# First tokens loaded in three contiguous pieces, one set of column means for two units, norm factors by a power on GpSimd, and a new order of the loads and of the opening's steps

## The chip, the cores and the metric

The kernel runs on one core of one Trainium2 chip. The time is the device time of one execution in microseconds (us); each kernel is run several times and medians are compared. The profile is one profiled execution. Engines are named as the profile names them: PE (matrix products) and PEld (its weight loads), DVE (vector), ACT (scalar and activation), POOL (GpSimd), SP (the queue that issues most transfers).

## The reference

For an input x of 2048 tokens and 448 channels the output is g·a + (1 − g)·b, with g a sigmoid of a weighted sum of each token's channels. Branch a is a state-space convolution along the tokens plus a skip term. Branch b is a mixer; its beginning is what this change touches:

```python
h = _gelu(_layernorm(x, axis=-1) @ w1)          # 448 x 448
c = D // 4
# the four quarters of h are shifted along the tokens by +1, -1, +2, -2
hs = jnp.concatenate([g0, g1, g2, g3], axis=-1) @ w2
x1 = x + hs
h2 = _gelu(_layernorm(x1, axis=-1) @ w3) @ w4   # 448 x 1792, 1792 x 448
return x1 + h2
```

`_layernorm` takes a token's mean and divides by sqrt(variance + 1e-5). Everything is float32.

## The kernel before

The 2048 tokens are worked on in four blocks of 512 (`TB`). Every float32 operand is split into a high part (the value rounded for PE's fast float32 form) and a low part (the rest), and a product is made of three products of parts: high·high, high·low and low·high.

A block's mixer has "units". The four units of the first layer (n = 0, 1, 2, 3 of block 0 are the quarters g = 0, 2, 1, 3 of `w1`'s columns) each multiply 448 channels, in four slices k of 128 rows (the last holds 64), into a PSUM tile; `first` at L478 issues these products. The norm is not applied to the tokens. Instead each column of `w1` has its mean over the channels taken out of it (`center`, L937), which removes the tokens' means, and the result is multiplied by the tokens' factors 1/sqrt(variance + eps) afterwards. The factors (`r1`) are one column of 128 tokens per tile; PE turns them into rows (`rows_of`, L363). Then come the gelu on ACT and the second layer (`second`, L603) into four accumulators `acc`. After that the 14 units of the 1792-wide layers follow for each block in the same two functions.

The opening is block 0's first layer. Here nothing has been loaded or split yet, so its steps are cut small and written out by hand in one table, `ORDER`; `begin` walks it and issues each step in turn, and every engine works through its own instructions in exactly that order. Words of the table that matter here:

- `m2`, `m0`, `m1`, `m3`: the column means of a quarter, as plain float32 matmuls of a constant 1/448 with the raw weights `w1r`, result in `pm`. `wt` and `ws` are sums on DVE (L922, L924, L910) of slices of quarters 2 and 0, made so that those means take two and three matmuls in place of four.
- `c2`: take the means out (DVE); `h2`: the high part (ACT, L940); `l2`: the low part (DVE, L943); the same for 0, 1, 3. Quarter 2 has only 64 columns, and its high and low parts lie side by side in `w1d`.
- `xha`, `xla`, `xhb`, `xlb`: high (ACT, L956) and low part (DVE, L961 and L963) of the tokens, left half (a) and right half (b) of the block.
- `p1:x0a`: a product of unit 1, low tokens (x), slice 0, left half; `h` stands for high by high, `l` for high tokens by low weights. Whole words such as `s0:10` are second-layer products.
- `w`: a warm-up product of constants (`pw`, L903).
- `sa0` to `sa6`, `sb2` to `sb9`: mean and variance of a token tile on ACT (two passes, L981 and L983) or on DVE (L974, L976). `ra0`, `ra1`: the factors of tiles 0 to 4 and 5 to 8; `ra`, `rm`, `rn`: their transposes on PE.
- `xz`, `pe`, `sk`: two edge tokens; `ld`: issue the later loads; `wh`, `wl`: the parts of `w2`.

The first loads are issued by `first_loads` on two queues, SP's and ACT's. The first tokens, transposed and with their margins, come from the array `x0`, whose 128 rows hold the left half and then the right half of all four slices; the kernel takes from it the left half's slices 0 and 1, its slices 2 and 3, and the right half. The parts of `w1` are called u0a and u0b (two halves of quarter 0), u2, u1 and u3 below.

The factors are computed by nine small DVE steps, a first guess by an integer trick and two refinements (`rstd_ops`, L317 to L333), for the tiles of the opening. For most later sets `rstd` makes two of the steps on DVE and ten on POOL (L344 to L353).

Of the kernel before, what the change touches and what calls it, by code (L numbers as in the profile page):

```python
# [179 lines left out]
def mixer_and_small_steps(ctx, tc, xs, gg, okm, x, xT, xb, x0, w1, w2, w3, w4, gate, par, logdt, dskip, ident, out):  # L180
# [25 lines left out]
    one = big.tile([128, 1], F32, name="one")  # L206
    carry = big.tile([128, 4, 5], F32, name="carry")
# [47 lines left out]
    def first_loads():  # L255

        r = raw[0] = room([128, 4 * XW], "raw")
        parts0.append(r[:, :4 * HW].rearrange("p (k t) -> p k t", k=4))
        parts0.append(r[:, 4 * HW:].rearrange("p (k t) -> p k t", k=4))
        act, sp = nc.scalar.dma_start, nc.sync.dma_start  # L260

        def load_w1(queue, g):
            t = slice(W1O[g], W1O[g] + 4 * (GD if g == 2 else 128))
            queue(w1r[:, t], w1[:, t])

        load_w1(act, 2)
        sp(r[:, :2 * HW], x0[:, :2 * HW])
        act(w1r[:, :256], w1[:, :256])  # L268
        sp(w1r[:, 256:512], w1[:, 256:512])
        act(xs[:, 0, :], x[0:128])  # L270
        sp(r[:, 2 * HW:4 * HW], x0[:, 2 * HW:4 * HW])
        load_w1(sp, 1)
        load_x(1, 2)
        load_x(2, 3)
        load_w1(sp, 3)
        load_x(3, 5)
        sp(r[:, 4 * HW:], x0[:, 4 * HW:])
        sp(idt, ident)
        sp(w2r[:, 0], w2[:, 0])  # L279
        load_xt(1)  # L280
        sp(w2r[:, 1:4], w2[:, 1:4])
        load_x(NT + 1, 2 * NT + 1)

    def constants():
# [3 lines left out]
        nc.gpsimd.memset(one, 1.0)  # L288
        nc.gpsimd.memset(nu, 0.0)
# [22 lines left out]
    def rstd_ops(r, j0, j1):  # L312

        v, t = (wk.tile([128, NT + 1], F32, name=n)[:, :j1 - j0] for n in "vt")
        y = r[:, j0:j1]
        stt = nc.vector.scalar_tensor_tensor
        nc.vector.tensor_scalar(v, st[:, j0:j1, 1], EPS, None, op0=OP.add)  # L317
        yield
        nc.vector.tensor_scalar(y.bitcast(I32), v.bitcast(I32), -0.5, float(0x5f3759df), op0=OP.mult, op1=OP.add)
        yield  # L320
        nc.vector.tensor_mul(t, y, y)
        yield
        stt(t, t, -0.5 * 0.375, v, op0=OP.mult, op1=OP.mult)
        yield
        stt(y, t, 1.5 * 0.375, y, op0=OP.add, op1=OP.mult)
        yield
        nc.vector.tensor_mul(t, y, y)
        yield
        stt(t, t, 1.0 / 0.140625, v, op0=OP.mult, op1=OP.mult)
        yield  # L330
        stt(t, t, -10.0 / 3.0, t, op0=OP.add, op1=OP.mult)
        yield
        stt(y, t, 5.0, y, op0=OP.add, op1=OP.mult)  # L333
        yield

    def rstd(r, j0, j1, eng=nc.vector):
        if eng is nc.vector:
            drain(rstd_ops(r, j0, j1))
            return
        v, t = (wk.tile([128, NT + 1], F32, name=n)[:, :j1 - j0] for n in "vt")  # L340
        y = r[:, j0:j1]
        nc.vector.tensor_scalar(v, st[:, j0:j1, 1], EPS, None, op0=OP.add)
        nc.vector.tensor_scalar(y.bitcast(I32), v.bitcast(I32), -0.5, float(0x5f3759df), op0=OP.mult, op1=OP.add)  # L343
        eng.tensor_mul(t, y, y)  # L344
        eng.tensor_mul(t, t, v)
        eng.tensor_scalar(t, t, -0.5 * 0.375, 1.5 * 0.375, op0=OP.mult, op1=OP.add)
        eng.tensor_mul(y, y, t)
        eng.tensor_mul(t, y, y)
        eng.tensor_mul(t, t, v)
        eng.tensor_scalar(t, t, 1.0 / 0.140625, -5.0 / 3.0, op0=OP.mult, op1=OP.add)  # L350
        eng.tensor_mul(t, t, t)
        eng.tensor_scalar(t, t, 20.0 / 9.0, None, op0=OP.add)
        eng.tensor_mul(y, y, t)  # L353

    def rstd2(j0, j1):
        rstd(r2, j0, j1, nc.gpsimd if j0 < 3 * NT else nc.vector)
# [475 lines left out]
    def mean_bank(g):  # L832
        pm[g] = ps.tile([128, GD if g == 2 else 128], F32, name="pm", tag=("misc", "acc2", "acc1", "acc3")[g], bufs=1)
        return pm[g]
# [28 lines left out]
    def col_means(g):  # L863
        p = mean_bank(g)
        for k in range(4):
            c = int(k == 3)
            nc.tensor.matmul(p, cm[:, c:c + 1].to_broadcast([128, 128]), W1R[g][:, k, :], start=k == 0, stop=k == 3)
# [36 lines left out]

    WS = {}

    def presum():

        WS[1] = big.tile([128, 128], F32, name="ws", tag="lt")
        nc.vector.tensor_add(WS[1], W1R[0][:, 0, :], W1R[0][:, 1, :])  # L910

    def presum_mean():
        a, p = W1R[0], mean_bank(0)
        for q, (c, r) in enumerate(((1, a[:, 3, :]), (0, a[:, 2, :]), (0, WS[1]))):
            nc.tensor.matmul(p, cm[:, c:c + 1].to_broadcast([128, 128]), r, start=q == 0, stop=q == 2)

    def presum_unit2():

        a = W1R[2]
        v = big.tile([128, GD], F32, name="ws", tag="yt")  # L920
        WS[0] = v
        nc.vector.tensor_add(v, a[:, 0, :], a[:, 1, :])  # L922
        yield
        nc.vector.tensor_add(v, v, a[:, 2, :])  # L924
        yield

    def unit2_mean():

        p = mean_bank(2)
        for q, c in enumerate((1, 0)):  # L930
# [371 lines left out]
```

## Time and profile before

| | us |
|---|---|
| median of 3 runs (lowest, highest) | 371.17 (371.15, 371.31) |
| span of the profiled execution | 368.9 |
| PE busy in that span | 363.4 |
| DVE, ACT, POOL busy | 308.1, 215.9, 63.3 |

The profile gives the span from the first to the last instruction of one execution and no device time of its own for that execution; the span stands 2.27 us below the median of the timed runs. A row of the timeline gives the start in us from the span's beginning, the duration, the engine, the kernel's line, the operation, what is written and read, and in brackets how long the engine was idle before and what released it. Matmuls are pipelined: their durations overlap, so the distance from one start to the next is what one costs.

### The profile page before, as it was taken

How to read it: one execution, taken by the hardware profiler on the slowest of the kernel's cores; microseconds unless marked ns; L12 is line 12 of the kernel's file. 1: busy time of each engine (PE TensorE's matmuls, PEld its weight loads, DVE VectorE, ACT ScalarE, POOL GpSimd, SP SyncE). 2: the span in 40 equal slices, each digit the busy share in tenths (PEclk: the TensorE clock that was granted, in tenths of full speed). 3: DMA queues.
4: the chain of work that ended last, by engine and by line, in shares of the span. 5: the costliest groups of instructions: out<-in, count | busy, mean ns of one | idle time of the engine just before them, and what ended most of it. 6: DMA issues, size and time to landing. Idle time of an engine off the chain costs nothing.

```text
span 368.9 us, 5308 instructions
## 1 busy us (share of the span) xinstructions
PE 363.4 (99%) x1734; PEld 314.3 (85%) x1734; DVE 308.1 (84%) x571; ACT 215.9 (59%) x383; POOL 63.3 (17%) x176
## 2 busy tenths in 40 slices
PE   8999999999999999999999999999999999999995
PEld 4988888888888888888888888888888888888885
DVE  4999979797999997378799899998789999998533
ACT  5987668777684637944274774554756645455220
POOL 1000432000300000110013433224243234000000
PEclk9999999999999999999999999999999999999999
DMA  7994116626948064001833514457385611361213
GB/s 258 393 398 157 38 65 124 134 88 251 390 134 203 0 116 156 0 0 52 178 107 77 89 28 94 114 165 131 83 131 121 179 16 28 79 179 30 64 50 105
DMA packets 88479, 46.14 MB, mean 125 GB/s; under 512 B 67200, under 2 KB 82944, under 8 KB 87808
## 3 DMA queue, kind: packets, MB, share of 16 engines
q1 hardware_dynamic: 88016, 45.27, 45.6%
q10 hardware_dynamic: 432, 0.49, 0.4%
q8 instruction: 15, 0.25, 0.3%
q14 instruction: 16, 0.13, 0.1%
HBM read 34.74 MB, written 11.01 MB: 124 GB/s over the span
## 4 chain that ended last, share of the span: by engine, by line
PE 93%; DMA 4%; ACT 1%; DVE 0%; ACTq 0%; SPq 0%; issue 0%
PE p L478 46%; PE acc L603 45%; DMA raw<-xb_in 2%; DMA xs<-x_in 2%; PE acc L638 1%; ACT xh L394 1%; PE p L638 0%; PE misc L363 0%; DVE xh L401 0%; ACT uf L996 0%; ACTq L268 0%; DVE uf L1007 0%; SPq L279 0%; ACT ug L1020 0%; ACT ug L1023 0%
## 5 line engine op out<-in xcount | busy, mean ns | idle before, releaser
L539 ACT ACTIVATE uf<-p 128x512 f32<-128x512 f32 x56 | 33.4, 597 | 113.3 <-PE p L478 113.2
L478 PE MATMUL p<-xh,w3l 128*128 128x512 f32 x224 | 70.1, 394 | 0.0
L478 PE MATMUL p<-xh,w3h 128*128 128x512 f32 x224 | 70.1, 394 | 0.0
L758 DVE TENSOR_TENSOR_SCAN z<-z,carry 128x512 f32<-128x512 f32 x48 | 61.5, 1282 | 4.2 <-POOL z L752 0.5
L603 PE MATMUL acc<-w4l,uh 128*128 128x448 f32 x216 | 56.3, 367 | 0.0
L603 PE MATMUL acc<-w4h,uh 128*128 128x448 f32 x216 | 56.0, 365 | 0.0
L603 PE MATMUL acc<-w4h,ul 128*128 128x448 f32 x216 | 55.8, 364 | 0.0
L569 DVE TENSOR_TENSOR ul<-uf,uh 128x512 fp32r<-128x512 f32 x56 | 38.1, 681 | 20.1 <-ACT uh L549 20.0
L478 PEld LDWEIGHTS p<-xh,w3l 128*128 128x128 f32 x224 | 42.1, 188 | 9.8
L478 PE MATMUL p<-xl,w3h 128*128 128x512 f32 x168 | 47.7, 392 | 0.0
L478 PEld LDWEIGHTS p<-xh,w3h 128*128 128x128 f32 x224 | 42.1, 188 | 6.6
L603 PEld LDWEIGHTS acc<-w4h,uh 128*128 128x128 f32 x216 | 40.5, 188 | 6.0
L603 PEld LDWEIGHTS acc<-w4h,ul 128*128 128x128 f32 x216 | 40.6, 188 | 3.5
L603 PEld LDWEIGHTS acc<-w4l,uh 128*128 128x128 f32 x216 | 40.6, 188 | 3.4
L753 ACT ACTIVATE z<-zs,nu 128x512 f32<-128x512 f32 x64 | 42.3, 710 | 0.6 <-DMA zs<-xT_in 0.6
L478 PEld LDWEIGHTS p<-xl,w3h 128*128 128x128 f32 x168 | 31.5, 188 | 7.2
L549 ACT ACTIVATE uh<-uf 128x512 fp32r<-128x512 f32 x56 | 35.4, 633 | 1.8
L752 POOL COPY z<-carry 128x1 f32<-128x1 f32 x48 | 32.1, 679 | 16.0 <-DVE zs L764 15.9
L760 POOL COPY carry<-z 128x1 f32<-128x1 f32 x48 | 13.1, 273 | 105.7 <-DVE z L758 105.0
L344 POOL TENSOR_TENSOR t<-r 128x4 f32<-128x4 f32 (+1 forms) x5 | 3.1, 627 | 117.4 <-DVE r L343 117.4
L603 PE MATMUL acc<-w2l,uh 128*128 128x448 f32 x64 | 19.9, 368 | 0.0
L758 DVE TENSOR_TENSOR_SCAN z<-z,carry,zero 128x512 f32<-128x512 f32 x16 | 19.9, 1247 | 0.0
(207 smaller groups left out, 541.8 us busy)
## 6 DMA issues: line engine op xcount, KB each, us to landing
zs<-xT_in SPq DMA_DIRECT2D x4, 1024.0 KB, 8.3
yd<-yt SPq DMA_DIRECT2D x56, 64.0 KB, 2.0
ysb<-yd SPq DMA_DIRECT2D x16, 224.0 KB, 2.7
raw<-xb_in SPq DMA_DIRECT2D x3, 1032.0 KB, 12.6
raw<-w_in SPq DMA_DIRECT2D x3, 1024.0 KB, 5.6
xd<-xt SPq DMA_DIRECT2D x16, 192.0 KB, 2.1
xr<-xd SPq DMA_DIRECT2D x16, 192.0 KB, 3.1
raw<-w_in SPq DMA_DIRECT2D x3, 896.0 KB, 4.6
```

The source lines that it names most:

```text
L344: eng.tensor_mul(t, y, y)
L394: nc.scalar.activation(XH["a", b][:, k, :], raw[b][:, k, :], AF.Copy)
L478: nc.tensor.matmul(p[:, t0:t1], (wl if w else wh)[:, k, :], (xl if x_ else xh)[:, k, o + t0:o + t1], start=(q == 0 and fresh), stop=stop i ...
L539: nc.scalar.activation(UF[n], P1[n], AF.Gelu_apprx_tanh)
L549: nc.scalar.activation(UH[n], UF[n], AF.Copy)
L569: nc.vector.tensor_sub(UL[n], uf, f32(UH[n]))
L603: nc.tensor.matmul(ACC[j], (UL if p == 2 else UH)[n][:, t], wl if p == 1 else wh, start=first_, stop=last_)
L638: nc.tensor.matmul(acc, (UL if p == 2 else UH)[m][:, t], (wl if p == 1 else wh)[:, c], start=q == last and m == n and p == 0, stop=m > n a ...
L752: nc.gpsimd.tensor_copy(z4[:, m, 0:1], carry[:, k, m:m + 1])
L753: nc.scalar.activation(z4[:, m, 1:], ZS[b][:, k, :], AF.Copy, scale=nu[:, k, m:m + 1])
L758: nc.vector.tensor_tensor_scan(z, z, up, carry[:, k, m:m + 1], OP.add, OP.add)
L760: nc.gpsimd.tensor_copy(carry[:, k, m:m + 1], z[:, TB - 1:])
```

## The change

1. `x0` is stored as three contiguous pieces (left half slices 0 and 1, left half slices 2 and 3, right half), each loaded whole. In the list of loads xa, xb, xc.
2. All loads of the opening are named in a table `LOADS` with the queue for each. SP now begins with u2, u0a, u0b, xc; ACT issues xa, xb and token tile 0.
3. The sums on DVE (`presum`, `presum_unit2`) go. Each set of means is again four matmuls, and quarters 1 and 3, which lie side by side in `w1r`, share one set of 256 columns.
4. The factors are made by two POOL instructions in all places: add eps, then raise to the power −0.5, with a constant tile `half`.
5. `ORDER` is written anew: left and right halves of units 1 and 0 come first, then units 2 and 3; more first-layer products stand ahead of the second layer.

```diff
+            w = (2 * HW, 2 * HW, 4 * (XW - HW))
+            return x0[sum(w[:q]) * 128:sum(w[:q + 1]) * 128].rearrange("(p t) -> p t", p=128)
...
+    LOADS = """
+    sp:u2 sp:u0a sp:u0b sp:xc act:xa act:xb sp:u1 sp:u3 sp:t2 sp:t3 act:t0 sp:v0 sp:t1 sp:n1 sp:id sp:v1 sp:t5
+    """
...
-        stt = nc.vector.scalar_tensor_tensor
-        nc.vector.tensor_scalar(v, st[:, j0:j1, 1], EPS, None, op0=OP.add)
...
+    def rstd(r, j0, j1):
         y = r[:, j0:j1]
+        nc.gpsimd.tensor_scalar(y, st[:, j0:j1, 1], EPS, None, op0=OP.add)
+        nc.gpsimd.tensor_tensor(y, y, half[:, :j1 - j0], OP.pow)
...
-    def col_means(g):
-        p = mean_bank(g)
+    def mean_ops(*gs):
+        p = mean_bank(gs)
         for k in range(4):
             c = int(k == 3)
-            nc.tensor.matmul(p, cm[:, c:c + 1].to_broadcast([128, 128]), W1R[g][:, k, :], start=k == 0, stop=k == 3)
+            w = W1R[gs[0]] if len(gs) == 1 else w1r[:, W1O[1]:].rearrange("p (i k m) -> p k i m", i=2, k=4)
+            nc.tensor.matmul(p, cm[:, c:c + 1].to_broadcast([128, 128]), w[:, k], start=k == 0, stop=k == 3)
+            yield
...
-    def presum():
...
-    def presum_unit2():
...
     ORDER = """
-    w w wt xha w wt m2 w xla m2 ws c2 m0 c2 h2 h2 l2 l2 p1:h0a c0 xha xz p1:x0a sk w xz sa0 xla p1:h2a m1 c0
+    ld m2 m2 m2 xha m2 m0 w w w c2 c2 h2 xla m0 h2 l2 l2 xha xla m0 m0 sk p1:x0a w w p1:x2a,h2a,x1a,h0a,h1a c0
...
```

Where the instructions stand, engine by engine. The names are those of the words above; line numbers of the changed kernel are its own (L444 is the first layer's product there, L837 the means, L329 the transposes of the factors, L318 and L319 the two steps of the factors).

SP's queue at the start, before:

```order
L267 DMA raw<-x_in 128x520
L269 DMA w1r<-w_in 128x256
L271 DMA raw<-x_in 128x520
L264 DMA w1r<-w_in 128x512
L246 DMA xs<-x_in 128x448 x2
L264 DMA w1r<-w_in 128x512
L246 DMA xs<-x_in 128x2x448
L277 DMA raw<-x_in 128x1024
```

and in the changed kernel, where L276 is u0a and u0b and L278 is xc:

```order
L269 DMA w1r<-w_in 128x256
L276 DMA w1r<-w_in 128x256 x2
L278 DMA raw<-x_in 128x1024
L269 DMA w1r<-w_in 128x512 x2
L272 DMA xs<-x_in 128x448
L272 DMA xs<-x_in 128x2x448
L281 DMA w2r<-w_in 128x448
L272 DMA xs<-x_in 128x448
```

The weights' parts moved ahead of the tokens, the left half's two pieces (128x520) went to ACT's queue, and the right half (128x1024) moved from behind the token tiles to ahead of quarters 1 and 3.

PE from the first means to the first products, before:

```order
L931 MATMUL pm<-w1r,cm 128x64
L903 LDWEIGHTS const-bfloat16-1.0
L903 MATMUL pw<-const-bfloat16-1.0 128x512
L931 MATMUL pm<-ws,cm 128x64
L915 MATMUL pm<-w1r,cm 128x128 x2
L915 MATMUL pm<-ws,cm 128x128
L478 MATMUL p_171<-xh,w1d 128x256
L478 MATMUL p_171<-xl,w1d 128x256
L903 LDWEIGHTS const-bfloat16-1.0
L903 MATMUL pw<-const-bfloat16-1.0 128x512
L478 MATMUL p_171<-xh,w1d 128x256
L867 MATMUL pm<-w1r,cm 128x128 x4
```

and in the changed kernel:

```order
L837 MATMUL pm<-w1r,cm 128x64 x4
L837 MATMUL pm<-w1r,cm 128x128
L874 LDWEIGHTS const-bfloat16-1.0
L874 MATMUL pw<-const-bfloat16-1.0 128x512
L874 LDWEIGHTS const-bfloat16-1.0
L874 MATMUL pw<-const-bfloat16-1.0 128x512
L874 LDWEIGHTS const-bfloat16-1.0
L874 MATMUL pw<-const-bfloat16-1.0 128x512
L837 MATMUL pm<-w1r,cm 128x128 x3
L444 MATMUL p_182<-xl,w1d 128x256
L874 LDWEIGHTS const-bfloat16-1.0
L874 MATMUL pw<-const-bfloat16-1.0 128x512
```

All of m0 now stands ahead of the first product, the two warm-ups behind it; one product stands there where two stood. On DVE in the same place, before:

```order
L922 TENSOR_TENSOR ws<-w1r 128x64
L924 TENSOR_TENSOR ws<-ws,w1r 128x64
L963 TENSOR_TENSOR xl<-raw,xh 128x2x260
L910 TENSOR_TENSOR ws<-w1r 128x128
L937 TENSOR_TENSOR w1r<-w1r,pm 128x128 x2
L943 TENSOR_TENSOR w1d<-w1r,w1d 128x2x64 x2
L937 TENSOR_TENSOR w1r<-w1r,pm 128x256
```

and in the changed kernel:

```order
L878 TENSOR_TENSOR w1r<-w1r,pm 128x128 x2
L904 TENSOR_TENSOR xl<-raw,xh 128x2x260
L884 TENSOR_TENSOR w1d<-w1r,w1d 128x2x64 x2
L904 TENSOR_TENSOR xl<-raw,xh 128x260
L878 TENSOR_TENSOR w1r<-w1r,pm 128x256 x2
L902 TENSOR_TENSOR xh<-raw,xh 64x260
```

The three sums are gone, and the first low part of the tokens (128x2x260) moved from ahead of `c2` (128x128 x2) to behind it.

POOL from the edge tokens on, before:

```order
L966 COPY xz<-raw 128x6
L850 MEMSET e 32x128
L968 COPY xz<-raw 64x2
L1003 MEMSET uf 128x1
L858 COPY skew<-e 16x1
L860 COPY skew<-e 16x2
L1003 MEMSET uf 64x2
L344 ISA
L344 TENSOR_TENSOR t<-r_80 128x4
L345 TENSOR_TENSOR t<-t,v 128x4
L346 TENSOR_SCALAR t<-t 128x4
```

and in the changed kernel:

```order
L907 COPY xz<-raw 128x6
L909 COPY xz<-raw 64x2
L318 ISA
L318 TENSOR_SCALAR r_80<-st 128x5
L319 TENSOR_TENSOR r_80<-r_80,half 128x5
L944 MEMSET uf 128x1
L944 MEMSET uf 64x2
L827 COPY skew<-e 16x1
L829 COPY skew<-e 16x2
```

The first arithmetic on POOL (L344, and the row ISA that sets POOL up for it) stood behind the edge tokens' last copies; now it stands right behind the first ones, ahead of the rows that need its result. Counted in PE's row, 63 first-layer products of 256 columns stand ahead of the factors' transposes now (62 before), and 79 of 256 and 12 of 512 columns ahead of the first second-layer product (77 and 4 before).

142 lines of the change are left out of this document (43 added, 99 removed).

## Prediction

> **What bounds the kernel now.** I read the page first: span, busy times, chain of waits.
>
> ```profile
> span 368.9 us, 5308 instructions
> PE 363.4 (99%) x1734; PEld 314.3 (85%) x1734; DVE 308.1 (84%) x571; ACT 215.9 (59%) x383; POOL 63.3 (17%) x176
> PEclk9999999999999999999999999999999999999999
> PE 93%; DMA 4%; ACT 1%; DVE 0%; ACTq 0%; SPq 0%; issue 0%
> ```
>
> PE is busy for 363.4 of 368.9 us at full clock and holds 93% of the chain; the rest of the chain is DMA, so it lies in the opening. Next the windows of the whole run, cut where the first real product starts and where the opening ends (columns: span, then busy us and instructions of PE, PEld, DVE, ACT, POOL).
>
> ```profile
> 0.00:6.71 6.71, 5.39 (x22) 2.60 (x22) 2.05 (x8) 2.63 (x5) 0.90 (x15) 1.00 0.68 213
> 6.71:12.37 5.66, 5.26 (x45) 4.75 (x46) 4.54 (x11) 4.85 (x14) 0.45 (x3) 1.00 1.04 368
> 12.37:22.00 9.63, 9.55 (x77) 8.90 (x74) 9.13 (x28) 8.54 (x20) 0.90 (x4) 1.00 1.03 406
> 22.00:360.00 338.00, 338.00 (x1570) 293.24 (x1569) 288.78 (x521) 199.93 (x346) 61.07 (x154) 1.00 0.44 112
> ```
>
> From 22 to 360 us PE never rests, and the change leaves the products of that stretch alone. So the time moves by what happens before the first product (6.71 us) and by PE's holes after it, plus any hole the change makes. The opening's timeline (start, duration, engine, line; in brackets idle time and its releaser):
>
> ```profile
> 0.73 0.41 ACTq L264 DMA_DIRECT2D w1r<-w_in  x1
> 0.74 0.40 SPq L267 DMA_DIRECT2D raw<-x_in  x1
> 1.65 0.43 SPq L271 DMA_DIRECT2D raw<-x_in  x1
> 4.22 0.64 ACT L956 ACTIVATE xh<-raw 128x520 fp32r<-128x520 f32 x1 [0.58 <-DMA raw<-x_in]
> 4.56 0.41 PE L931 MATMUL pm<-w1r,cm 128*128 128x64 f32 x2 [0.17 <-DMA w1r<-w_in]
> 4.88 0.70 DVE L963 TENSOR_TENSOR xl<-raw,xh 128x520 fp32r<-128x520 f32 x1
> 4.80 0.38 PE L903 MATMUL pw<-const-bfloat16-1.0 128*128 128x512 bf16 x1
> 5.02 0.40 PE L931 MATMUL pm<-ws,cm 128*128 128x64 f32 x2
> 5.26 0.66 PE L915 MATMUL pm<-w1r,cm 128*128 128x128 f32 x4
> 5.71 0.48 DVE L937 TENSOR_TENSOR w1r<-w1r,pm 128x128 f32<-128x128 f32 x2
> 6.36 0.49 DVE L943 TENSOR_TENSOR w1d<-w1r,w1d 128x128 fp32r<-128x128 f32 x2 [0.18 <-ACT w1d L940]
> 6.71 0.39 PE L478 MATMUL p<-xh,w1d 128*128 128x256 f32 x1 [0.38 <-DVE w1d L943]
> 6.93 0.28 PE L478 MATMUL p<-xl,w1d 128*128 128x256 f32 x1
> 7.06 0.39 PE L903 MATMUL pw<-const-bfloat16-1.0 128*128 128x512 bf16 x1
> 7.16 0.64 ACT L956 ACTIVATE xh<-raw 128x520 fp32r<-128x520 f32 x1 [0.63 <-DMA raw<-x_in]
> 7.83 0.43 DVE L963 TENSOR_TENSOR xl<-raw,xh 128x260 fp32r<-128x260 f32 x1 [0.64 <-ACT xh L956]
> 7.85 0.39 PE L478 MATMUL p<-xh,w1d 128*128 128x256 f32 x1 [0.40 <-ACT xh L956]
> 8.26 0.40 ACT L940 ACTIVATE w1h<-w1r 128x256 fp32r<-128x256 f32 x1
> 9.67 1.15 PE L867 MATMUL pm<-w1r,cm 128*128 128x128 f32 x8
> 13.70 0.51 PE L478 MATMUL p<-xh,w1h 128*128 128x256 f32 x3
> 20.43 0.52 PE L478 MATMUL p<-xh,w1l 128*128 128x256 f32 x2
> 21.02 0.67 PE L603 MATMUL acc<-w2h,uh 128*128 128x448 f32 x2
> ```
>
> The first product waits for the chain u2, means, c2, h2, l2. The third waits for the second piece of tokens, landed just ahead of 7.16: 0.79 us from 7.06 to 7.85 with one warm-up in it. A product of 256 columns takes 0.117 us of PE's row (13.70: three in 0.51, of which the last one's drain is 0.28 as at 6.93), one of 512 columns twice that. After the two that start at 20.43 the next instruction was due by 20.78 at the latest and came at 21.02. Those are PE's holes, about 1.1 us together. More than that, beside an earlier first product, cannot be won.
>
> **The change, part by part.** I add it up against this profile's span of 368.9; the runs' median, 371.17, lies 2.27 us above it, which I carry over unchanged.
>
> *First product.* u2 now leads SP, and the first piece of tokens leads ACT. A piece twice u2's size at the head of SP landed by 4.22, so I take 4.1 for u2. Its means are now four matmuls instead of two and no sums on DVE: 0.24 each (5.02 to 5.26), so 4.15 to 5.1, ended at 5.3, and c2 starts there instead of 5.71. But DVE's 0.70 us xl step, which at 4.88 filled the wait, now stands behind c2: c2 5.30 to 5.75, xl to 6.37, first l2 done at 6.66, product at 6.70. The 0.4 us won on the presums is spent on that step. In PE's row, m0's last matmuls stand ahead of the product and want u0b, third on SP. Its bounds: 1.65 plus the fastest landing of a w1 piece, and the third SP piece of now (7.16).
>
> ```profile
> DMA to landing us min/median/max: 3.6/3.8/5.7
> ```
>
> That is 5.25 to 7.16; I take the middle, 6.2, because half the bytes ride in it but as many are ahead. A plain fp32 matmul of 128 columns is two passes of 0.11 (the row at 9.67: eight in 1.15 with the drain), so three end at 6.9. **First product: +0.19 us.** The Trainium skill's page "DMA: Bandwidth & Descriptors", section "Queues, rings and completion order", says each DMA engine takes turns between queues packet by packet; by that, SP's 1 KB packets fall behind ACT's 2 KB ones and u0b would come after both token pieces, nearer the late bound.
>
> *The hole at 7.06.* The second piece is now second on ACT, issued near 1.17 instead of 1.65; I take 6.2 as well (4.7 at the fastest, 7.16 at the slowest). Its high part is done at 6.85, the third xl step at 7.3, while PE is in two warm-ups (0.22 each, 4.80 to 5.02) until 7.45. So no wait there; the five products end at 8.05. c0 follows that xl step (0.41 and then ACT's 0.40) and lets unit 0 start at 8.15: 0.1 of wait and 0.1 of restart. Before: 0.79 plus 0.11 of restart. After: 0.43 plus 0.2. **−0.27 us.**
>
> *One set of means for units 1 and 3.* Sixteen passes of 128 columns become eight of 256. No row has a plain fp32 pass of 256 columns; it costs between 0.12 (the fp32r one) and 0.22 (two of the narrow). A pass seems to cost by its columns (0.11 at 128), so I take 0.22: **0**, at best −0.8. u3 must be there: the row at 9.67 shows it landed by then, with about as many bytes ahead as now, and PE comes to this set near 10.3.
>
> *The hole at 20.8.* It belongs to the first second-layer product, which waits for ACT. In the new row 79 products of 256 and 12 of 512 columns stand ahead of that product, before 77 and 4. Eight more at 0.23 put it 1.8 us later, behind the same wait. **−0.35 us.**
>
> *The power.* Two POOL instructions replace nine on DVE (first set, 15.36 to 17.13) and, later, ten on POOL.
>
> ```profile
> 15.36 0.16 DVE L317 TENSOR_SCALAR v<-st 128x5 f32<-128x5 f32 x1
> 16.97 0.17 DVE L333 SCALAR_TENSOR_TENSOR r<-t,r 128x5 f32<-128x5 f32 x1
> 13.38 0.65 ACT L983 ACTIVATE xn<-xs,st 128x448 f32<-128x448 f32 x1
> 27.04 0.30 DVE L976 BATCH_NORM_AGGREGATE st<-b 128x2 f32<-128x6 f32 x2
> L349 POOL TENSOR_TENSOR t<-t,v 128x3 f32<-128x3 f32 x1 | 0.7, 748 | 0.1
> 47.72 0.57 POOL L344 TENSOR_TENSOR t<-r 128x4 f32<-128x4 f32 x1 [3.11 <-DVE r L343]
> 50.65 0.20 POOL L353 TENSOR_TENSOR r<-r,t 128x4 f32<-128x4 f32 x1
> ```
>
> No row has a power. It is one instruction on 5 values a partition: no less than 0.20 us (L353), no more than the ten-step chain that it replaces (47.72 to 50.85, 3.1 us). I take 0.75, the dearest plain instruction of that size (L349) and near the middle by ratio. PE wants the factors for its row transposes after 63 products: 6.9 + 63 × 0.117 + 0.43 + 1.76 of means + 0.6 of small ones and restarts = 17.1. The statistics end on ACT at about 16.25 (from 7.7: two w1 parts, two token parts, six statistic passes of 0.56 or 0.65, two w1 parts of 0.63, one w2 part, one copy, 7.6 us, and 1 us of waiting for the joint means). Then 0.2 for the sum, 0.75, and two hand-overs of 0.1: 17.4. **+0.3.** At the second set the last aggregate moves from 27.2 to between 28.1 and 29.2 (four steps of 0.6 to 0.7 moved ahead of it, nine of 0.2 gone), and PE's next row transposes stand at about 30.2: 29.2 + 1.15 gives **+0.1**, or nothing. Later sets have units of time to spare; DVE's saving there is hidden, as PE is the bound.
>
> *Three contiguous pieces.* The bytes and the row lengths moved are the same; I cost it at nothing, with the landings' bounds above.
>
> Sum: +0.19 − 0.27 − 0.35 + 0.40 = −0.03. **Span 368.9, time 371.1: no change.**
>
> **Rivals.** A measurement of this kernel tells about 0.2%, 0.74 us, from no change.
>
> 1. *The power is dear, slower.* It stands in PE's path twice: the first hole is p − 0.45, the second p − 0.6. Against −0.43 from the rest, the time is over 0.74 us worse from p = 1.1 us. At 1.5 us the sum is −0.43 + 1.9 = +1.5: 372.6; at 3.1 it is 375.8. For it: POOL runs this in steps, and its plain instructions vary from 0.20 to 0.75 already. Chance 0.2.
> 2. *u0b lands as late as the third SP piece does now.* m0 ends at 7.9, first product +1.16, while the waits of 0.2 behind it go: 371.1 + 0.75 = 371.9. Chance 0.1.
> 3. *The pieces come early and the power is cheap.* u0b at 5.25 frees PE at 6.7 (DVE's chain then sets it), no wait at 8.15, power 0.2: −0.01 − 0.45 − 0.35 = −0.8: 370.3. Chance 0.15.
> 4. *The first power pays for POOL's set-up.* The row ISA ahead of POOL's first arithmetic stood between 20.05 and 39.62, hidden; now it follows the copies of the first tokens, near 6.5, and the sum wants POOL at 16.3. A set-up beyond 9.8 us would show, up to 9.8 us: 381. If it is paid at the first call, the first L344 call shows 0.5 us (0.69 against 0.20): 371.6. Chance 0.05.
>
> ```profile
> 20.05 0.09 POOL L1003 MEMSET uf<- 64x2 f32 x1 [0.94 <-DVE uf L491]
> 39.62 0.69 POOL L344 TENSOR_TENSOR t<-r 128x4 f32<-128x4 f32 x1 [19.47 <-DVE r L343]
> ```
>
> The Trainium skill's "GPSIMD Engine Reference", section "Instruction dispatch", gives about 5.95 us for the first call of a freshly loaded kernel. Counted from the set-up, that is hidden here as it was at 39.62, where the trace agrees; counted at the call, an estimate by that page is 376 to 377.
>
> **How the numbers follow.** My forecast (370.4 to 371.8) has 0.5, the rivals 0.2, 0.1, 0.15 and 0.05. Faster by over 0.2%: rival 3 and 0.05 of the forecast, 0.2. Slower: rival 1, most of 4 and a part of 2, 0.28. Within: 0.52. The range 370.2 to 372.9 leaves out part of rival 3, the dear half of 1, and 4.
>
> **What would show it.** After: first product at 6.9 and PE busy from 8.3 on; the L837 means of 256 columns at 0.2 us a pass; no idle time ahead of the first second-layer product; the duration of POOL L319, and whether PE's transposes (L329) wait for it. Wrong if u0b or the power are far from 6.2 and 0.75.

## Result and the profile after

| | before | after |
|---|---|---|
| median of 6 runs (lowest, highest), us | 371.25 (371.15, 372.04) | 375.67 (374.27, 376.32) |
| ratio, 95% interval | 1 | 1.0111 (1.0098 to 1.0124) |
| profiled execution: time, span | span 368.9 | 374.44, span 372.6 |

The change makes the kernel 1.1% slower; no change had been forecast. After's six times stand in two groups, 374.27 to 375.09 and 376.25 to 376.32, and the profiled execution is of the first. Every ratio below is against runs of the kernel before on the same chip. One timed run of less_warm_up_before and the profiled execution of half_in_one were disturbed (more than twice the usual time) and are left out. The page of after, to be held against the page rows shown of before:

```profile
span 372.6 us, 5234 instructions
PE 365.2 (98%) x1732; PEld 314.5 (84%) x1732; DVE 303.3 (81%) x531; ACT 215.8 (58%) x383; POOL 61.8 (17%) x143
PEclk9999999999999999999999999999999999999999
PE 92%; DVE 3%; DMA 1%; POOL 1%; ACT 1%; issue 1%; SPq 0%
```

PE is still the bound, but POOL and DVE now have a share in the chain. The view of waits says where PE stands still (line waiting, what for, total, times, longest):

```profile
PE misc L329 <- POOL r L319: 1.3, 1, 1.3
PE misc L329 <- POOL uf L944: 0.7, 1, 0.7
PE pm L837 <- DMA w1r<-w_in: 0.2, 1, 0.2
```

Both long waits are those of the row transposes, L329. The windows (columns as for before) show that they lie in the two stretches of the two sets of factors, and that from the first product at 7.07 up to 33 us PE idles nowhere else:

```profile
0.00:7.07 7.07, 6.00 (x27) 3.29 (x27) 1.66 (x6) 3.16 (x6) 1.36 (x19) 1.00 0.71 239
7.07:12.37 5.30, 5.30 (x38) 4.87 (x37) 3.57 (x9) 4.32 (x12) 0.00 (x0) 1.00 1.05 394
12.37:22.00 9.63, 8.91 (x73) 8.25 (x73) 8.00 (x19) 7.92 (x18) 2.42 (x6) 1.00 1.04 403
22.00:29.50 7.50, 7.50 (x38) 6.26 (x37) 7.39 (x16) 6.42 (x17) 0.00 (x0) 1.00 1.03 390
29.50:33.00 3.50, 2.17 (x13) 1.64 (x13) 2.05 (x6) 1.30 (x3) 1.92 (x2) 1.00 0.41 150
```

The timeline at the places that the prediction spoke of:

```profile
6.60 0.52 PEld L837 LDWEIGHTS pm<-w1r,cm 128*128 128x128 f32 x4 [0.27 <-DMA w1r<-w_in]
7.07 0.36 PE L444 MATMUL p<-xl,w1d 128*128 128x256 f32 x1
10.48 1.89 PE L837 MATMUL pm<-w1r,cm 128*128 128x256 f32 x8
16.46 0.19 ACT L924 ACTIVATION_READ_ACCUMULATOR xn<-xs,st 128x1 f32 x1
16.74 0.26 POOL L318 TENSOR_SCALAR r<-st 128x5 f32<-128x5 f32 x1 [11.15 <-ACT xn L924]
17.08 1.20 POOL L319 TENSOR_TENSOR r<-r,half 128x5 f32<-128x5 f32 x1
18.31 0.24 DVE L821 TENSOR_SCALAR e<-pe,r 2x32 f32<-2x32 f32 x1 [1.50 <-POOL r L319]
18.33 0.76 PE L329 MATMUL misc<-idt,r 128*128 128x128 f32 x5 [0.72 <-POOL uf L944]
30.06 0.30 DVE L917 BATCH_NORM_AGGREGATE st<-b 128x2 f32<-128x6 f32 x2
30.45 0.51 POOL L318 TENSOR_SCALAR r<-st 128x4 f32<-128x4 f32 x1 [9.10 <-DVE st L917]
31.04 1.41 POOL L319 TENSOR_TENSOR r<-r,half 128x4 f32<-128x4 f32 x1
32.51 0.65 PE L329 MATMUL misc<-idt,r 128*128 128x128 f32 x4 [1.33 <-POOL r L319]
```

The power is L319: 1.20 and 1.41 us. At 18.33 the releaser is named as the fill L944, which stands behind the power on POOL; the power had ended at 18.28. DVE waits too: its first step for the edge tokens (L821) needs the factors and stands still for 1.50 us, with everything behind it on DVE late.

PE's last matmul starts at 364.94 before and at 368.00 after, 3.06 us later. What follows it in the span, 3.99 and 4.57 us, lies between 3.9 and 4.7 in all nineteen profiles, whatever the kernel, and is left out of the account below.

### The profile page after: what moved, and what is told of

Its sections match the earlier page's. It is cut to its first block, busy times and chain, and to the rows that moved or that the text cites. A ratio compares the mean times of both kernels' runs of the same rounds, so it can differ in the third digit from the quotient of the medians.

```text
span 372.6 us, 5234 instructions
## 1 busy us (share of the span) xinstructions
PE 365.2 (98%) x1732; PEld 314.5 (84%) x1732; DVE 303.3 (81%) x531; ACT 215.8 (58%) x383; POOL 61.8 (17%) x143
## 4 chain that ended last, share of the span: by engine, by line
PE 92%; DVE 3%; DMA 1%; POOL 1%; ACT 1%; issue 1%; SPq 0%
PE p L444 46%; PE acc L569 43%; DMA w1r<-w_in 1%; PE acc L604 1%; POOL r L319 1%; PE pm L837 1%; DVE b L915 1%; DVE w2l L884 0%; PE p L604 0%; DVE xl L365 0%; PE misc L329 0%; DVE uf L475 0%; DVE w1r L878 0%; POOL r L318 0%; DVE uf L948 0%
## 5 line engine op out<-in xcount | busy, mean ns | idle before, releaser
L444 PE MATMUL p<-xh,w3h 128*128 128x512 f32 x224 | 70.8, 397 | 0.0
L444 PE MATMUL p<-xh,w3l 128*128 128x512 f32 x224 | 70.0, 393 | 0.0
L444 PEld LDWEIGHTS p<-xh,w3l 128*128 128x128 f32 x224 | 42.2, 188 | 10.2
L444 PE MATMUL p<-xl,w3h 128*128 128x512 f32 x168 | 48.1, 395 | 0.0
L444 PEld LDWEIGHTS p<-xh,w3h 128*128 128x128 f32 x224 | 42.0, 188 | 6.7
L444 PEld LDWEIGHTS p<-xl,w3h 128*128 128x128 f32 x168 | 31.6, 188 | 7.6
L318 POOL TENSOR_SCALAR r<-st 128x4 f32<-128x4 f32 (+2 forms) x8 | 5.0, 620 | 134.3 <-DVE st L307 103.9
L569 PE MATMUL acc<-w2h,uh 128*128 128x448 f32 x64 | 19.9, 370 | 0.0
```

Of the source, the lines that this page charges most:

```text
L318: nc.gpsimd.tensor_scalar(y, st[:, j0:j1, 1], EPS, None, op0=OP.add)
L444: nc.tensor.matmul(p[:, t0:t1], (wl if w else wh)[:, k, :], (xl if x_ else xh)[:, k, o + t0:o + t1], start=(q == 0 and fresh), stop=stop i ...
L569: nc.tensor.matmul(ACC[j], (UL if p == 2 else UH)[n][:, t], wl if p == 1 else wh, start=first_, stop=last_)
```

## The experiments: the power and its place

**no_power** and **free_factors**. The power left out, and both factor instructions replaced:

```diff
-        nc.gpsimd.tensor_scalar(y, st[:, j0:j1, 1], EPS, None, op0=OP.add)   # stays in no_power
-        nc.gpsimd.tensor_tensor(y, y, half[:, :j1 - j0], OP.pow)
+        nc.gpsimd.memset(y, 1.0)                                             # free_factors only
```

> The changed kernel without the power instruction: the factors are only variance plus eps, so this kernel's norms are not those of the reference; all else stays. Theory A, the power stands in PE's path at both sets of row transposes (1.20 us at 17.08, 1.41 us at 31.04 in the changed kernel's trace) and that is where the time went: the sum alone ends at 17.0 and 30.96, ahead of PE at 17.45 and 31.0, so both holes go (0.88 + 1.50 = 2.4 us), time 373.3, ratio to before 1.0055. Theory C, most of the loss is elsewhere (the slower beat of PE after 150 us, the wider spread of the runs): below 1 us is won, time 375. Theory D, the power also slows VectorE or ScalarE beside it: more than 2.4 us is won, 372 or less.

> The changed kernel with both factor instructions replaced by one constant fill that waits for no statistics (the norms are left out, the statistics are still taken). Theory A: no more than the power leaves, both holes closed, 373.3, equal to the kernel without the power within 0.3 us, as the sum alone is no longer waited for. Theory B, what is late are the statistics and not the power (the last aggregate moved from 27.34 to 30.36, while PE's rows stand at 31.0): this kernel wins clearly more than the one without the power, since there the sum of 0.5 us and two hand-overs still stand in the path: 0.5 us more. Theory C: 375.

Measured: no_power 372.3 (371.02 to 373.48), ratio 1.0037 (1.0022 to 1.0052); free_factors 373.41 (372.82 to 373.77), 1.0057 (1.0044 to 1.0070). Rows of no_power's timeline:

```profile
17.05 0.24 DVE L820 TENSOR_SCALAR e<-pe,r 2x32 f32<-2x32 f32 x1 [0.22 <-POOL r L318]
29.14 0.30 DVE L916 BATCH_NORM_AGGREGATE st<-b 128x2 f32<-128x6 f32 x2
30.10 0.64 PE L328 MATMUL misc<-idt,r 128*128 128x128 f32 x4
365.37 0.27 PE L603 MATMUL p<-w4h,ul 128*128 128x128 f32 x1
```

Without the power neither PE nor DVE waits for the factors, the last aggregate comes at 29.14 in place of 30.06, and PE ends 2.63 us sooner than in after (368.00 to 365.37). So the power costs 2.6 us where it stands: 0.9 at the first set, 1.5 at the second, and 0.2 in a small wait at 81. Theory A holds for the amount, 2.6 us against its 2.4; the time fell somewhat further than it had said (1.0037 against 1.0055). free_factors' span of 371.0 is longer than no_power's though less is waited for; that led to the section on the half rate. From the first product to the last matmul PE takes 358.42 us in free_factors and 358.38 in no_power, so leaving out the sum as well won nothing there, again as Theory A expected.

**before_power** and **old_factors**. The new factors in the old order, and the old factors in the new order:

```diff
 # before_power, in place of the steps of rstd_ops and rstd
+        nc.gpsimd.tensor_scalar(y, st[:, j0:j1, 1], EPS, None, op0=OP.add)
+        nc.gpsimd.tensor_tensor(y, y, half[:, :j1 - j0], OP.pow)
 # old_factors, in ra0 and ra1: those two lines out, the nine DVE steps in
```

> The kernel before with only the factors changed: sum and power on GpSimd in place of the nine VectorE steps and the ten-step chain, at the place of the first of them; order and loads untouched. Theory A in its strict form, the power is too slow for this place wherever it stands: holes of about 1 us, 372.2 or more. Theory B, the place decides: in the order of before the first set's statistics end at 14.8 and PE's rows come at 17.5, so sum and power (1.6 us) end by 16.6; at the second set 27.4 + 2.1 = 29.5 against 31.9. No hole, VectorE gets 2 x 1.7 us back: 371.2, at best 0.3 less where VectorE is waited for at 20.8.

> The changed kernel with the old factors: nine VectorE steps in one piece where sum and power stood at the first two sets, the ten-step GpSimd chain later; new order, loads and means stay. Theory A, the power is what was lost: the time falls towards before, 373.5 or less. Theory B, in the new order the statistics come too late for any chain: nine steps of 0.2 us are 1.8 us against 1.6 to 2.1 for sum and power, and they now also hold VectorE: holes as long as now (0.9 and 1.2 to 1.5 us), time 375 to 376.5.

Measured: before_power 371.84 (371.01 to 372.07), ratio 1.0012 (1.0003 to 1.0020); old_factors 376.63 (376.31 to 378.01), 1.0152 (1.0133 to 1.0171). First before_power's two factor instructions, then the nine steps' first and last and the transposes in old_factors:

```profile
14.60 0.26 POOL L321 TENSOR_SCALAR r<-st 128x5 f32<-128x5 f32 x1 [6.88 <-ACT xn L952]
14.94 1.51 POOL L322 TENSOR_TENSOR r<-r,half 128x5 f32<-128x5 f32 x1
```

```profile
18.39 0.17 DVE L321 TENSOR_SCALAR v<-st 128x5 f32<-128x5 f32 x1 [0.44 <-ACT xn L962]
20.00 0.17 DVE L337 SCALAR_TENSOR_TENSOR r<-t,r 128x5 f32<-128x5 f32 x1
20.22 0.76 PE L367 MATMUL misc<-idt,r 128*128 128x128 f32 x5 [0.91 <-DVE r L337]
```

In the old order a power of 1.51 us ends at 16.45, a microsecond ahead of PE's transposes at 17.43, and is free. In the new order even the old steps make PE wait, 2.0 us in all. Theory B: the new order takes the statistics so late that any factor chain stands in the path. In after, sum and power (16.74 to 18.28, 1.54 us) are even a little shorter than the nine steps (18.39 to 20.17).

**rows_later** and **stats_earlier**. Only `ORDER` is edited:

```diff
-... rm ra p2:h3b,h0a p5:h0 p3:l0b sk mu0 p4:l0 p3:l0a ...   ra1 rn bn s3:10 wl3 s3:21 uf5 tl3 s3:31,02,22 cp3
+... p2:h3b,h0a p5:h0 p3:l0b sk p4:l0 p3:l0a rm ra mu0 ...   ra1 s3:10 wl3 s3:21 uf5 tl3 s3:31,02,22 rn bn cp3   # rows_later
-... p0:l2b,h3b wh0 pe p2:h1b,x2a,h2a,h0b sa1 uf1 sa1 p2:h1a uf0 ...
+... p0:l2b,h3b pe p2:h1b,x2a,h2a,h0b sa1 sa1 uf1 p2:h1a wh0 uf0 ...                                             # stats_earlier
```

> The changed kernel with PE's row transposes moved back in PE's own order: at the first set behind six products (0.9 us), at the second behind five second-layer groups; VectorE's, ScalarE's and GpSimd's orders stay. If the place and not the power is what costs, the products fill both holes while the power runs: 0.9 + 1.5 us won, 373.3, as without the power, and no new wait, since the rows then come no later than they did. If something behind the rows (their multiplies, the rows' copy by ScalarE) was already late, the hole only moves: less than 1 us won, 375.

> The changed kernel with one move in ScalarE's order: the two statistic steps of token tile 1 stand together, ahead of the copy of unit 1's sums (0.59 us) and of the high part of unit 0's second weights (0.56 us), which followed w1's and stood ahead of them. The statistics then end 1.15 us sooner (15.5 in place of 16.65), sum and power at 17.1. In the changed kernel VectorE too waits 1.50 us for the factors, in its first skew step, and everything on VectorE behind it is late, the last aggregate among it (30.36). Theory B, late statistics start both holes: both go or nearly, 1.5 to 2.4 us won, 373.3 to 374.2. If the second hole has its own cause (the power alone, 1.41 us there): only the first 0.9 us is won, 374.8.

Measured: rows_later 375.11 (373.67 to 375.63), ratio 1.0104 (1.0085 to 1.0123); stats_earlier 375.1 (373.72 to 375.99), 1.0109 (1.0094 to 1.0124). Neither won what Theory B had promised. Two rows of rows_later, then two of stats_earlier:

```profile
18.55 0.24 DVE L821 TENSOR_SCALAR e<-pe,r 2x32 f32<-2x32 f32 x1 [1.51 <-POOL r L319]
23.19 0.50 PE L444 MATMUL p<-xl,w1d 128*128 128x512 f32 x1 [0.60 <-DVE xl L365]
```

```profile
16.31 0.18 DVE L917 BATCH_NORM_AGGREGATE st<-b 128x2 f32<-128x6 f32 x1
16.67 0.26 POOL L318 TENSOR_SCALAR r<-st 128x5 f32<-128x5 f32 x1 [11.36 <-ACT uf L455]
```

In rows_later PE no longer waits at the first transposes, but DVE still stands 1.51 us at L821, so the low parts of the next tokens are late and PE waits for those. In stats_earlier ACT's statistics ended at 15.96, but DVE's last aggregate at 16.49 now held the sum (the row names ACT's copy L455, which writes nothing that the sum reads). The second hole stayed at 1.3 us. Each edit moved one of two waits that end almost together.

**after_placed** and **after_placed2**. DVE's statistics of tiles 3 and 4 go into its idle time ahead of `c1` and ACT's as in stats_earlier; tiles lie as in after_layout (next section). after_placed also moves the second set's statistics ahead of `wl1`, `rn` a little back, and adds a warm-up; after_placed2 moves `rn` as rows_later does.

```diff
-... m1 m1 m1 c1 c3 ...  sa1 uf1 sa1 p2:h1a uf0 sb3 l1 sb3 p3:x1b l3 sb3 p2:x0b sb3 ...
+... m1 m1 m1 sb3 sb3 c1 c3 ...  sa1 sa1 uf1 p2:h1a wh0 uf0 sb3 sb3 l1 p3:x1b l3 p2:x0b ...
-... wl1 s2:21 hd3 sk hd3 s2:12,01 p4:h0 sb5 hd3 sb7 cp3 s1:01 sb5 p4:l3 sb7 ra1
+... sb5 sb7 sb5 sb7 ra1 wl1 s2:21 hd3 sk hd3 s2:12,01 p4:h0 hd3 cp3 s1:01 p4:l3        # after_placed only
```

> The changed kernel with the power kept and its place mended: VectorE's statistics of tiles 3 and 4 and ScalarE's of tile 1 earlier in the first set (VectorE idled 1.34 us there for the means), the last aggregates of the second set ahead of the low part of unit 1's second weights, PE's second row transposes behind three more second-layer groups; one more warm-up matmul; tiles as in after_layout. Theory B, the place and not the power was what cost: first hole gone (sum at 15.9, power done by 17.3, rows wanted at 17.45), second down from 1.5 to 0.5 or less, so 1.9 to 2.4 us and 0.7 of the beat won: 372.0 to 373. Theory A, the power's length costs wherever it stands in this order: holes of 0.7 and 1.3 stay, 374.5.

> The changed kernel with the power kept, the first set's statistics earlier on VectorE and ScalarE, PE's second row transposes behind five more second-layer groups, and the tiles as in after_layout. Theory B: both holes gone or under 0.4 us, beat as before; 0.9 + 1.2 + 0.7 = 2.8 us off the changed kernel. What is left is the opening at half rate: in ten profiles with this opening the first product starts at 7.0 to 7.8 (five) or 8.7 to 8.9 (five), 1.7 us apart: times near 371.5 and near 373.2, median 372.4, ratio 1.003. Theory A: 374 or more.

Measured: after_placed 373.73 (373.15 to 375.36), ratio 1.0058 (1.0038 to 1.0078); after_placed2 373.53 (373.27 to 373.93), 1.0067 (1.0053 to 1.0081). PE's waits in after_placed, then in after_placed2:

```profile
PE acc L571 <- ACT uh L517: 1.4, 1, 1.4
PE acc L571 <- DVE w2l L886: 0.5, 1, 0.5
```

```profile
PE misc L331 <- POOL r L321: 0.2, 1, 0.2
PE acc L571 <- ACT uh L514: 0.2, 1, 0.2
PE pm L839 <- DMA w1r<-w_in: 0.2, 1, 0.2
```

In both the first hole is gone with the power in place: place, not length, made it. after_placed paid for its second move: the power now stood ahead of a skew copy on POOL, ACT waited 2.6 us for that copy, and PE for ACT. after_placed2 is left with 0.2 us at the second set and 0.2 us on ACT behind it. It missed the forecast median of 372.4. Its profile is of the late kind described below, with the first product at 8.77, and 373.2 had been expected for that kind; its five times lie within 0.66 us, but that all five are late was not traced.

## The experiments: where the tiles lie

The change adds a tile of five columns for the exponent, `half`. In the first profiles with it PE's beat (the distance from one start to the next) in the long stretch differed from before: eleven products of 512 columns took 2.58 us in half of the stretch. These are pieces of the chain (start, us, line, count) of after, then of after_layout:

```profile
147.86 2.55 PE p L444 x11
162.86 2.58 PE p L444 x11
```

```profile
149.34 2.55 PE p L446 x11
164.31 2.55 PE p L446 x11
```

I summed, from 85 to 360 us, what each start-to-start distance takes beyond 0.2305 us (512 columns) or 0.203 (448): 0.85 us before, 1.54 after. Five kernels change addresses; the two whose names begin with before_power also have the power in the old order:

```diff
+    half = big.tile([128, NT + 1], F32, name="half")     # before_half: filled, never read
-    one = big.tile([128, 1], F32, name="one")            # half_in_one, before_power_half_in_one
+    one = big.tile([128, 8], F32, name="one")
+    one, half = one[:, 0:1], one[:, 1:2 + NT]
+        for n in "vt":                                   # besides that, in *_layout: the old steps'
+            wk.tile([128, NT + 1], F32, name=n)          # two tiles stay allocated
```

> The kernel before with one thing added: the tile of five columns that holds the exponent, and its fill; nothing reads it. It moves the tiles that are allocated behind it by 20 bytes. In all five profiles of kernels with this tile PE's first products of a unit take 30 ns more from 150 to 220 and from 290 to 363 us (0.08 us lost in 10 us against 0.02 before), 0.8 us in all. Theory G, the tile's place does it: the same beat here, ratio 1.002, 372.0. Rival H, it comes with the power or the other parts of the change: 371.2 and the beat of before.

> The changed kernel, but the exponent's five columns lie in the unused rest of the slot of the tile of ones, so that every tile behind it starts at the address that it has in the kernel before (a multiple of 64 bytes for the token tiles, as before; 32 bytes further in the changed kernel). Theory G, the place of the tiles sets PE's beat: the beat of before from 150 to 220 and 290 to 363 us (0.02 to 0.03 us lost in 10 us, not 0.08), 0.8 to 1.2 us won, 374.6. Rival H, it came with something else of the change: 375.7, beat unchanged.

> The kernel before with the power in place of the old factors, the exponent in the free rest of the slot of the tile of ones, so no tile moves but those that the old factors no longer need. Theory B, the place decides whether the power is waited for: no hole at either set, and the 0.37 us at the first second-layer product are won, since VectorE no longer has the nine steps. With theory G the beat of before: 370.9, ratio 0.998 to 0.999. If the beat stays slow although the addresses are those of before: 371.7.

> The kernel before with the power, and every tile at its address in the kernel before: the exponent in the rest of the slot of ones, and the two small tiles of the old factors still allocated though unused. Theory G2, PE's beat from 80 us on goes with the addresses (four layouts so far, each with a beat of its own): the beat of before, 0.02 to 0.03 us lost in 10 us throughout, and with the 0.37 us won at 20.8 us: 370.9, ratio 0.999. Rival H2, the beat goes with the instructions of GpSimd and VectorE and not with addresses: slow beat somewhere, 371.8 or more.

> The changed kernel with the same two steps, so that the tiles that PE reads lie as in the kernel before (a few that PE does not read, of the norms and of the first sums, do not). Theory G2: the beat of before, 0.7 us won on the changed kernel, 374.9 by the median, both holes unchanged. Rival H2: beat of 0.08 us in 10 us in half of the stretch, 375.6.

| kernel | time (lowest, highest) | ratio (interval) | sum of the beat, us |
|---|---|---|---|
| before_half | 372.30 (371.90, 372.92) | 1.0033 (1.0021 to 1.0045) | 1.91 |
| half_in_one | 374.83 (374.50, 376.75) | 1.0107 (1.0090 to 1.0124) | no profile |
| before_power_half_in_one | 372.35 (371.99, 372.98) | 1.0027 (1.0016 to 1.0038) | 1.84 |
| before_power_layout | 371.18 (370.43, 371.56) | 0.9989 (0.9977 to 1.0001) | 0.88 |
| after_layout | 375.09 (373.59, 375.82) | 1.0084 (1.0059 to 1.0108) | 0.88 |

The tile of 20 bytes takes a slot of 32. Though nothing reads it there, it made the kernel before 0.33% slower (before_half). Theory G in its first form (the 32 bytes alone) fell with before_power_half_in_one: the tokens' tiles were back, but the old factors' small tiles were gone and `uf`, `uh` and `ul` (the gelu's values and their parts) had moved by 128 bytes, and the beat was slow in the other half of the stretch. With all tiles that PE reads at their old addresses it came back. Over the nineteen profiles those with the same placement agree within 0.03 us: 0.85 to 0.88 in eight with before's, 1.52 to 1.55 in eight with after's (before_power is one), 1.91 in two, 1.84 in one. So the placement costs after 0.69 us by the beat; the times of after_layout and after alone do not tell them apart (1.0084 and 1.0111, intervals that overlap). The slots and moves of tiles are worked out from the kernels' allocations; no trace shows an address. Why some addresses are slower was not found.

## The experiments: the half rate of the opening

The granted clock reads 1.00 from the first window on. Yet PE's steps start at half rate (a warm-up 0.427 us apart, later 0.216), and the moment when they double differs. The same instructions in after, then in free_factors:

```profile
4.13 1.52 PE L837 MATMUL pm<-w1r,cm 128*128 128x64 f32 x10 [0.22 <-DMA w1r<-w_in]
5.49 0.81 PE L874 MATMUL pw<-const-bfloat16-1.0 128*128 128x512 bf16 x3
```

```profile
4.05 2.48 PE L836 MATMUL pm<-w1r,cm 128*128 128x64 f32 x10
6.32 1.49 PE L873 MATMUL pw<-const-bfloat16-1.0 128*128 128x512 bf16 x3
8.74 0.56 PE L443 MATMUL p<-xl,w1d 128*128 128x256 f32 x1
```

In after the steps' rate doubled near 4.5 us, in free_factors near 9.2, and its first product came 1.67 us later. Over the eleven profiles with the new opening the first product starts at 6.98 to 7.30 (four), 7.80 (more_warm_up_after) or 8.66 to 8.85 (six). With the old opening, eight profiles, it starts at 6.71 to 7.31. The Trainium skill's page "TensorE: Matmul & The Clock Gate", section "What's actually happening", says that PE's clock is halved until one window of about 3.4 us has been busy, and that the windows run freely, so that the moment differs from run to run. The traces agree that steps are twice as long at first and that the moment varies. The range is not explained by one busy window alone: the rate doubled at 3.4 us in before, 2.7 us after PE's first matmul at 0.77, and at 9.5 in warm_between, 8.7 us after it. Three kernels ask what in the opening decides it:

```diff
-    w w wt xha w wt m2 w xla m2 ws c2 m0        # less_warm_up_before
+    wt xha wt m2 w xla m2 ws c2 m0
-        warm_up(7)                              # more_warm_up_after
+        warm_up(9)
-    ld m2 m2 m2 xha m2 m0 w w w c2 c2           # warm_between
+    ld m2 w m2 w m2 w xha m2 m0 c2 c2
```

> The kernel before without the three warm-up matmuls between the first seven and the first means; PE then idles from 3.7 to about 4.5 as the changed kernel's does from 3.7 to 4.1. In the profiles so far PE's steps halve (warm-up 427 to 216 ns) at 3.4 to 4.8 us, but at 9.1 us in two kernels with the changed kernel's opening, which costs 1.7 us there. Theory E, the idle time and the thin means in it put that moment off in some executions: this kernel's times spread as the changed kernel's do, some at 371 and others at 372.5 to 374, median over 372. Rival F, the moment is by chance alone or comes from the loads: as before, 371.2 with a spread under 1 us.

> The changed kernel with nine warm-up matmuls ahead of the first means in place of seven; they end at 4.56 at half rate, so the means start up to 0.45 us later. Theory E: fewer executions keep the half rate to 9.1 us, the cluster at 376.3 thins out, median 374.5 to 375. Rival F: all times move up by 0.2 to 0.4 us, both clusters stay, median 376.

> The changed kernel with the three warm-up matmuls behind the first means moved between them (a warm-up behind each of the first three k steps of unit 2's means), no matmul more or less. In the six profiles with this opening PE's steps halve at 4.3 to 4.8, 6.4, or 9.0 to 9.1 us, in those with the opening of before by 5.3 at the latest; a gap of 0.8 us in the opening of before did not put it off. Theory E2, the thin means in a row (eight passes of 64 columns and two of 128, 1.7 to 2.1 us at half rate) count as little work and keep the half rate: with warm-ups between them the moment comes by 6 us, no times near 376.3, median 374.5 to 375. Rival F, chance alone: times spread from 374.3 to 376.5 as now, median 375.7 or later by the delay of the means (0.2 to 0.6 us).

Measured: less_warm_up_before 371.35 (371.00 to 372.04), ratio 1.0005 (0.9994 to 1.0016); more_warm_up_after 374.75 (373.61 to 375.39), 1.0088 (1.0068 to 1.0107); warm_between 374.62 (373.85 to 376.56), 1.0093 (1.0074 to 1.0112). The idle time alone did not do it in the old opening (Theory E falls in that form), nor do thin means in a row explain it: warm_between's profile kept the half rate to 9.5 with warm-ups between them (E2 falls). With nine warm-ups the median was within Theory E's 374.5 to 375, no time was above 375.39, and in their profile the doubling came at 6.4, but the means start 0.4 us later; six times and one profile do not show that fewer executions are late. So the new opening is open to a late doubling that costs 1.7 us, and the old one, in eight profiles, never showed a first product later than 7.31; what sets the moment stays open. After's second group of times lies 1.8 us above the first (medians 376.27 and 374.44); that it is this late kind fits the size but was not traced.

## The experiments: the pieces, and the best version

```diff
-        sp(r[:, :2 * HW], x0[:, :2 * HW])
+        sp(r[:, :2 * HW], x0_part(0))           # and the other two pieces, and x0's order in device memory
```

> The kernel before with the first tokens in three contiguous pieces in device memory and nothing else changed (queues and order of the loads as before). By the prediction's step, the same bytes in the same rows on the SBUF side cost the same: 371.3, ratio within 0.1%, third product still waits 0.4 us for the second piece. Rival: contiguous source rows land sooner (second piece by 6.8 in place of 7.13): up to 0.3 us won.

> The kernel before with the power at unchanged addresses and the contiguous pieces together, order and queues as before. If the two small gains add up (0.4 us each: 0.37 at the first second-layer product, 0.4 at the third product's wait for the second piece): 370.6, ratio 0.9975, faster than both kernels. If they are the same gain or by chance: 0.999, 371.1.

Measured: before_pieces 371.09 (370.31 to 372.29), ratio 0.9985 (0.9972 to 0.9998), barely clear of no change. before_power_pieces, which adds the power at before's addresses, 370.58 (369.86 to 371.31), 0.9982 (0.9970 to 0.9994): faster than both kernels, though the two gains do not add up to what was expected. The issues of the first tokens' first two pieces (count, KB, median us to landing) in before_power_layout, where they are strided, and in before_power_pieces:

```profile
raw<-x_in SPq DMA_DIRECT2D x2, 260.0 KB, 4.4
```

```profile
raw<-x_in SPq DMA_DIRECT2D x2, 260.0 KB, 3.7
```

In six profiles with strided pieces the second one landed at 6.93 to 7.39 us, in the two with contiguous ones at 5.73 and 5.80, with the same bytes ahead of it on the same queues.

## Why the prediction was wrong, point by point

- **First product**, forecast 6.9: 7.07, or 8.7 in the late kind. u0b landed at 6.56 where 6.2 was taken (PE's weight loads wait for it up to 6.60), behind token pieces that landed at 4.19 and 5.15. The Trainium skill's "DMA: Bandwidth & Descriptors", section "Queues, rings and completion order", had spoken for that order, and the trace agrees; but u0b was also issued after both pieces (1.66 against 0.73 and 1.16), so the turns between queues are not shown by it. Rival 2, 7.16, did not come. In the profiled execution u0b's landing is the term that was off. In the late kind it is the rate: every price was taken at full rate, PE's means at half rate last until 8.7, and no term stood for that.
- **The hole at 7.06**, forecast −0.27 and PE busy from 8.3: held, as far as there is no wait from 7.07 to 12.37; its size was not measured apart.
- **Joint means**, 0.22 a pass: eight in 1.89 us with the drain are 0.215 each. Held.
- **The hole at 20.8**, forecast −0.35: no wait is left there. Held.
- **The power**, forecast 0.75, +0.4 in all: 1.20 and 1.41, and 2.63 us on the path. This is the step that failed, in three parts. First, the power was sized at little more than half its length, on a misread row: L349's 0.748 us is not the dearest plain POOL instruction of that size in before. Its timeline also has this one:

```profile
97.35 1.10 POOL L344 TENSOR_TENSOR t<-r 128x4 f32<-128x4 f32 x1 [31.70 <-DVE r L343]
```

Its 1.10 us is the length from which rival 1 expects a loss that can be told from noise. By the step's own rules the first hole is 1.20 − 0.45 = 0.75, measured 0.88 with the hand-overs between the engines, and the second 1.41 − 0.6 = 0.81, measured 1.5. Second, the sum at the second set took 0.51, not 0.2. Third, the last aggregate came at 30.36, not 29.2. Without the power it ended at 29.44, so most of this delay is the power's own: DVE waits 1.50 us for the factors at L821, and the prediction asked who waits for POOL and named PE alone.
- **Rival 1** named the mechanism rightly and gave it 0.2. With the measured lengths its formula makes −0.43 + 0.75 + 0.81 = +1.1 us, 372.3, so it too was far short: it lacks what DVE's wait does to the second hole, the placement and the late kind. **Rival 4** did not happen: the first power took 1.20 us, a later one 1.41, and the 0.69 us of the first L344 call was no sign of a set-up, since a later call took 1.10. The estimate by the Trainium skill's "GPSIMD Engine Reference", section "Instruction dispatch", 376 to 377, lay near the result by luck: no call of 5.95 us is in the trace.
- **Contiguous pieces**, costed at nothing: in the old order the second one lands 1.3 us sooner, and the three win 0.15% by themselves.
- **Not seen at all**: the placement of tiles, +0.69 us.

The account of PE's 3.06 us in the profiled execution: power +2.63 (368.00 against 365.37 in no_power), placement +0.69, all the rest −0.26. That rest is what the change was worth with the power out of the path, in executions whose half rate ends early. The medians differ by 4.42 us: besides the 3.06 there are 0.58 us behind the last matmul, within the scatter of that stretch, and 0.8 us that go with after's second group of times.

## What to carry to other kernels

Before a cheaper instruction sequence goes to another engine, list every engine that waits for its result, and read from the trace when its inputs are ready and when each reader wants it: here the same power was free in one order and cost 2.6 us in the other. Compare PE's start-to-start beat, not only its waits: a tile that nothing read cost 0.33% and shows in no view of waits. Where PE itself bounds the opening, as in the late kind here, its microseconds at half rate become part of the time and of its spread.

## What was not expected of the hardware

- A power on POOL over three to five values a partition takes 1.04 to 1.73 us (eight in after); the plain arithmetic instructions of that size on POOL take 0.20 to 1.11 us there, and one and the same line (L318, four values) 0.23 to 1.11.
- The start addresses of tiles in SBUF change PE's beat by up to 30 ns in 2.55 us, in some stretches and not in others, the same in every profile with the same placement.
- PE's half rate at the start ended between 3.4 and 9.5 us while the granted clock read 1.00.
- The second transfer of the same rows landed 1.3 us sooner when its source was contiguous.
